# A training-step kernel on one Trainium2 core: the opening reordered, layer-norm statistics six rows ahead instead of eight, and mask products made four wide ones

## The chip, the core and the metric

The kernel runs on one core of one Trainium2 chip. The metric is the device time of one execution in microseconds (us). A measurement has several runs of a kernel, and beside them runs of the kernel before on the same chip. The granted clock is the share of full speed that TensorE was given, as the profile records it; half clock is 0.5. The span in a profile, from the first instruction to the last, is 1 to 3 us shorter than the time of the same run.

## The reference

The kernel computes the output of a two-part layer and the gradients of all its inputs. Only the first part matters here (shortened): layer norm, a two-dimensional FFT, a product with a complex weight, and the inverse FFT.

```python
def _A_ref(x, w_r, w_i):                       # x: 2048 x 448
    X = rfft2(x.astype(float32), axes=(-2, -1))
    X = X * (w_r + 1j * w_i)
    return irfft2(X, s=(S, D), axes=(-2, -1)).astype(bfloat16)

h  = x + _A_ref(_layernorm(x), w_r, w_i)
h2 = h + _B_ref(_layernorm(h), w1, b1, w2, b2) # two matrix products and a gelu
...
_out, _vjp = jax.vjp(_f, A_x, A_w_r, A_w_i, B_w1, B_b1, B_w2, B_b2)
return (_out, *_vjp(grad_out))
```

## The kernel before

FFTs are done as matrix products with tables of sines and cosines. The kernel opens with a *row stage*: a loop over 16 tiles of 128 rows of x. For each tile, VectorE needs the mean and variance of the rows (`ln_stats`), a table scaled by their reciprocal standard deviation (`scale_R`, tile `rX`), and the sums and differences of the row's halves (`fold_prep`, tile `rS`, two rows at a time). With these TensorE does a row product (`row_a`), and four iterations later a second one (`row_b`). Products of grad_out with w2 (`fill`) stand in between, so that TensorE has work while VectorE prepares the next row. They need only loads.

The reciprocal root for rows 6 to 15 is a chain of ten small operations on GpSimd, for two rows at a time:

```python
def newton_gp(v, y, sl):
    ...
    gp_.tensor_scalar(out=v, in0=v, scalar1=LN_EPS, scalar2=None, op0=ALU.add)
    gp_.tensor_scalar(out=yi, in0=v.bitcast(I32), scalar1=-0.5, scalar2=RSQRT_MAGIC, op0=ALU.mult, op1=ALU.add)
    for c0, c1 in RSQRT_STEPS:
        gp_.tensor_tensor(out=a, in0=y, in1=y, op=ALU.mult)
        gp_.tensor_tensor(out=a, in0=a, in1=v, op=ALU.mult)
        gp_.tensor_scalar(out=a, in0=a, scalar1=c0, scalar2=c1, op0=ALU.mult, op1=ALU.add)
        gp_.tensor_tensor(out=y, in0=a, in1=y, op=ALU.mult)
```

Two tables say in which iteration `t` the statistics of a row (`STATS`) and the GpSimd root of a pair (`GROUPS`) are issued. In the kernel before the statistics of row t+8 are issued in iteration t:

```python
GROUPS = {0: (6, 8), 1: (8, 10), 3: (10, 12), 5: (12, 14), 7: (14, 16)}
STATS = {0: (6, 7), 1: (8, 9), **{t: (t + 8,) for t in range(2, 8)}}
...
for t in range(NT):
    ...
    if t + 1 < NT:
        row_a(t + 1, Rs.pop(t + 1))
    fill(FILL_A[t])
    if 1 <= t and t + 3 < NT:
        ...
        Rs[t + 3] = scale_R(t + 3)
    row_b(t - 3)
    ...
    if t % 2 and t < 12:
        fold_prep(xn, t // 2 + 2)
    for i in STATS.get(t, ()):
        ln_stats(xn, i, mvx)
    for _ in range(3 if t > 0 else 0):
        if next(uv, None):                     # a piece of the group tables
            break
    if t in GROUPS:
        a, b = GROUPS[t]
        newton_gp(mvx[:, a:b, 1], rstd_x[:, a:b], slice(a, b))
    ...
    fill(FILL_B[t])
```

The tables for the next stage (`Ut`, `Vt`) are also made during this loop. Each column is multiplied by a mask, in eight narrow products per table, on whichever of VectorE and ScalarE has less work by the kernel's own account:

```python
for j in range(4):
    m = msk[:, j:j + 1]
    dj = d1[:, :, :, j - 1] if j else dst[:, :, 112:128]
    for o, c in ((d0[:, :, :, j], 0), (dj, 1)):
        if load[1] + 0.24 < load[0] + 0.38:
            ve.tensor_scalar(out=o, in0=cv[:, :, :, c], scalar1=m, scalar2=None, op0=ALU.mult)
        else:
            sc.activation(out=o, in_=cv[:, :, :, c], func=ACT.Copy, scale=m)
        yield
```

## Time and profile before

| | before |
|---|---|
| median time | 356.7 us (356.2 to 357.64, 3 runs) |
| span of the profiled run, mean granted clock | 355.7 us, 0.989 |
| row product of row 4 starts | 19.97 us |
| row product of row 14 starts | 40.85 us |
| first product of the stage after (permI with Vt) starts | 50.37 us |

The last rows come from the timeline of TensorE. The busy shares, the windows and the waits of the kernel before stand in the prediction. Columns are start, time, engine, line, operation, output and inputs, and the number of instructions; a bracket gives the idle time just before and what ended it. ScalarE's timeline of before:

```profile
28.26 1.93 ACT L82 ACTIVATE Ut<-rO,cols 128x256 bf16<-128x256 bf16 x3
29.93 0.69 ACT L82 CAST rS<-ps_ff 128x512 bf16<-128x512 f32 x1
```

TensorE's timeline of before, at the same time:

```profile
30.67 0.57 PE L218 MATMUL ps_ff<-csF,rS 112*128 112x226 bf16 x4 [1.62 <-ACT rS L82]
```

Three mask products in a row hold ScalarE for 1.93 us. The copy of a row product out of PSUM, which the program also names `rS`, stands behind them, and TensorE waits 1.62 us for it.

GpSimd's timeline of before, from the last reciprocal root (rows 14 and 15), which begins at 32.97 us:

```profile
33.33 0.29 POOL L1174 TENSOR_SCALAR stats<-mvx 128x16 f32<-128x16 f32 x1
33.68 0.33 POOL L1176 TENSOR_SCALAR stats<-mvx 128x16 f32<-128x16 f32 x1
...
36.30 0.19 POOL L388 TENSOR_TENSOR rstd_x<-nt_f,rstd_x 128x2 f32<-128x2 f32 x1
```

### The profile page before, as it was taken

To read this page: it belongs to the slowest core of one execution; us is meant where nothing else is said; L and a number is where in the kernel's file an instruction comes from. 1 tells how busy PE (TensorE), PEld (TensorE's weight loads), DVE (VectorE), ACT (ScalarE), POOL (GpSimd) and SP (SyncE) were. 2 spreads that over 40 slices of the span, in tenths; PEclk is the share of its full clock that TensorE was granted. 3 is DMA by queue.
4 is the path that set the end of the run, shared out by engine and by line. 5 is a ranking of instruction groups with operands and counts; after the bars stand their busy time and mean duration, and the time that the engine had idled before them with its cause. 6 is when DMAs were issued, how large, how long until landed. Compare 5 with 4: busy or idle time off the path is not lost.

```text
span 355.7 us, 6447 instructions
## 1 busy us (share of the span) xinstructions
PE 341.0 (96%) x2133; PEld 183.8 (52%) x2133; DVE 254.5 (72%) x680; ACT 213.6 (60%) x457; POOL 69.1 (19%) x227
## 2 busy tenths in 40 slices
PE   5888999999999999999999999999999999999995
PEld 2345765555645555555555555544454544565542
DVE  5797638981884888776235888786595965499993
ACT  4549848965986545504222345566387866579872
POOL 8667100000221000001001111110000000067860
PEclk9699999999999999999999999999999999999999
DMA  8999969758999999977777999989966898799995
GB/s 209 272 186 211 235 172 184 161 163 284 280 292 357 299 350 237 251 218 222 183 186 150 190 213 189 216 151 300 292 180 194 231 232 248 228 203 265 245 282 218
DMA packets 147672, 81.62 MB, mean 229 GB/s; under 512 B 95480, under 2 KB 139768, under 8 KB 147384
## 3 DMA queue, kind: packets, MB, share of 16 engines
q1 hardware_dynamic: 147352, 80.83, 91.5%
q10 hardware_dynamic: 288, 0.39, 0.3%
q8 instruction: 16, 0.26, 0.3%
q14 instruction: 16, 0.13, 0.2%
HBM read 27.56 MB, written 23.89 MB: 145 GB/s over the span
## 4 chain that ended last, share of the span: by engine, by line
PE 73%; DVE 8%; ACT 7%; DMA 5%; issue 2%; SPq 2%; POOL 0%; DVEq 0%; ACTq 0%
PE ps_mm L218 61%; PE ps_ff L218 12%; DVE r L82 4%; DMA out_dram<-rG 2%; ACT rO L82 2%; DMA rB<-in_A_w_i_dram 2%; ACT rG L82 2%; DVE stats L82 2%; DMA rA<-in_A_x_dram 2%; SPq L297 1%; ACT Ut L82 1%; DVE rA L82 1%; DVE rS L82 1%; ACT rX L82 1%; ACT Vt L82 1%
## 5 line engine op out<-in xcount | busy, mean ns | idle before, releaser
L218 PEld LDWEIGHTS <-r 128*128 128x128 bf16 (+1 forms) x660 | 61.8, 104 | 49.6 <-issue 2.5
L218 PEld LDWEIGHTS <-rS 128*128 128x128 bf16 (+2 forms) x496 | 40.5, 98 | 38.3 <-issue 5.9
L218 PE MATMUL ps_mm<-rD,r 128*128 128x448 bf16 x224 | 44.5, 352 | 0.0
L82 ACT CAST rO<-ps_mm 128x512 bf16<-128x512 f32 (+1 forms) x66 | 35.2, 579 | 11.3 <-PE ps_mm L218 10.8
L218 PE MATMUL ps_mm<-rC,rE 128*128 128x448 bf16 x144 | 35.9, 370 | 3.6 <-DMA rC<-in_grad_out_dram 3.6
L218 PEld LDWEIGHTS <-rst 128*128 128x128 bf16 (+1 forms) x320 | 23.8, 97 | 29.0 <-issue 13.7
L218 PE MATMUL ps_mm<-r,rst 128*128 128x512 bf16 (+3 forms) x192 | 36.5, 353 | 0.0
L82 ACT CAST r<-ps_ff 128x452 bf16<-128x452 f32 x56 | 31.8, 575 | 7.6 <-PE ps_ff L218 7.4
L218 PE MATMUL ps_mm<-rB,r 128*128 128x448 bf16 x160 | 31.2, 352 | 0.1
L218 PE MATMUL ps_mm<-rG,rst 128*128 128x512 bf16 (+1 forms) x128 | 28.4, 380 | 0.0
L82 ACT ACTIVATE r<-ps_mm,rstd_h 128x448 bf16<-128x448 f32 x16 | 10.1, 633 | 26.8 <-PE ps_mm L218 26.8
L82 ACT ACTIVATE r<-rC 128x448 bf16<-128x448 bf16 x16 | 9.1, 571 | 26.7 <-DMA out_dram<-r 21.6
L82 DVE SCALAR_TENSOR_TENSOR r<-ps_mm,b2col,r 128x448 bf16<-128x448 f32 x16 | 10.9, 683 | 19.9 <-PE ps_mm L218 18.4
L82 ACT ACTIVATE rG<-rG 128x896 bf16<-128x896 bf16 x14 | 13.3, 950 | 14.9 <-DVE rG L82 14.7
L218 PEld LDWEIGHTS <-rO 128*128 128x128 bf16 (+1 forms) x165 | 15.6, 98 | 11.5 <-DMA rO<-in_B_w_dram 1.1
L218 PE MATMUL ps_mm<-rE,rS 128*128 128x448 bf16 x112 | 21.5, 352 | 0.0
L1182 POOL TENSOR_SCALAR lcol<-lcol 128x1 f32<-128x1 f32 x16 | 8.5, 530 | 64.7 <-ACT r L82 64.7
L218 PEld LDWEIGHTS <-rE 128*128 128x128 bf16 x148 | 14.4, 101 | 12.3 <-issue 5.6
L218 PE MATMUL ps_mm<-rC,rO 128*128 128x448 bf16 x80 | 19.1, 352 | 0.8 <-DMA rO<-in_B_w_dram 0.8
L1373 POOL TENSOR_SCALAR lcol<-lcol 128x1 f32<-128x1 f32 x16 | 4.7, 296 | 77.0 <-ACT r L82 76.9
L218 PE MATMUL ps_ff<-csI,rAT 113*128 113x224 bf16 (+1 forms) x108 | 19.0, 298 | 0.6 <-ACT rAT L82 0.4
L82 ACT CAST rG<-ps_mm 128x512 bf16<-128x512 f32 (+1 forms) x28 | 14.4, 550 | 8.1 <-PE ps_mm L218 8.0
(197 smaller groups left out, 661.0 us busy)
## 6 DMA issues: line engine op xcount, KB each, us to landing
out_dram<-rO SPq DMA_DIRECT2D x34, 256.0 KB
r<-in_B_w_dram SPq DMA_DIRECT2D x5, 1024.0 KB
r<-r SPq DMA_DIRECT2D x16, 226.0 KB
r<-r SPq DMA_DIRECT2D x32, 113.0 KB
rS<-in_B_w_dram SPq DMA_DIRECT2D x4, 896.0 KB
out_dram<-rG SPq DMA_DIRECT2D x10, 256.0 KB
rO<-in_B_w_dram SPq DMA_DIRECT2D x2, 1024.0 KB
w_d<-rG SPq DMA_DIRECT2D x1, 1808.0 KB
```

The costliest lines, as they stand in the source:

```text
L82: fn(**kw)
L218: nc.tensor.matmul(out, lhsT=lhsT, rhs=rhs, start=start, stop=stop)
L297: nc.sync.dma_start_transpose(out=wT, in_=B_w2[j * P:(j + 1) * P, :].rearrange("f (t c) -> f t c", c=P))
L1182: gp_.tensor_scalar(out=m1, in0=ms, scalar1=-1.0 / D, scalar2=None, op0=ALU.mult)
L1373: gp_.tensor_scalar(out=m1, in0=ms, scalar1=-2.0 / D, scalar2=None, op0=ALU.mult)
```

## The change

Its intent: have the sine tables and the first statistics done sooner, keep TensorE's clock up with more idle matmuls, issue the statistics later so that VectorE, which is full from 20 to 31 us, gets to the tables and folds of the next rows first, and take the mask products off ScalarE.

```diff
-    for _ in range(12):
+    for _ in range(26):
         nc.tensor.matmul(idle[:, 0:D], lhsT=rAT[:, 0:P], rhs=rAT[:, 0:D], start=True, stop=True)
 ...
-            for j in range(4):
-                m = msk[:, j:j + 1]
-                ...
+            for out, c, j in ((d0, 0, 0), (d1, 1, 1)):
+                n = 4 - j
+                load[1] += 0.06 + 256.0 * n / 960.0
+                nc.vector.tensor_tensor(out=out, in0=cv[:, :, :, c:c + 1].broadcast_to([P, 16, 16, n]),
+                                        in1=mskb[:, 0:1, 0:1, j:4].broadcast_to([P, 16, 16, n]), op=ALU.mult)
+                yield True
+            evac_mask(dst[:, :, 112:128], cv[:, :, :, 1], msk[:, 0:1])
+            yield
 ...
-    for fn in fwd_ops[:4]:
+    for fn in fwd_ops:                 # both sine tables before the first statistics
         fn()
 ...
-    GROUPS = {0: (6, 8), 1: (8, 10), 3: (10, 12), 5: (12, 14), 7: (14, 16)}
-    STATS = {0: (6, 7), 1: (8, 9), **{t: (t + 8,) for t in range(2, 8)}}
+    GROUPS = {0: (6, 8), 3: (8, 10), 5: (10, 12), 7: (12, 14), 9: (14, 16)}
+    STATS = {0: (6, 7), **{t: (t + 6,) for t in range(2, 10)}}
 ...
-    FILL_A = (3, 3, 3, 3, 3, 3, 3, 3, 3, 3, 3, 3, 3, 3, 3, 3)
-    FILL_B = (3, 3, 3, 3, 3, 3, 3, 3, 3, 3, 3, 3, 3, 3, 3, 3)
+    FILL_A = (4, 4, 4, 3, 3, 4, 4, 4, 4, 4, 4, 3, 3, 3, 3, 3)
+    FILL_B = (0, 0, 0, 3, 3, 3, 3, 3, 3, 3, 3, 3, 3, 3, 3, 3)
```

Cut from this: the load of x rows 2 and 3 goes ahead of the first part of grad_out, `fold_prep` of rows 2 and 3 and the identity go ahead of row 0, and four fills stand before row 0 in place of six after it.

More of the change, by code (lines that the diff above doesn't have):

```diff
@@ L310 @@
     load_w2T()
+    nc.sync.dma_start(out=xn[:, 2:4, :], in_=x_pt[:, 2:4, :])
     load_go(0)
-    nc.sync.dma_start(out=xn[:, 2:4, :], in_=x_pt[:, 2:4, :])
     load_go(1)
@@ L463, with evac_mask @@
     comp_ring = ring(rO, 0, 2, 512)
+    mskb = mem.tile([P, 1, 1, 4], BF16, name="mskb")
+    def evac_mask(out, in_, m):
+        if load[1] + 0.43 < load[0] + 0.7:
+            ve.tensor_scalar(out=out, in0=in_, scalar1=m, scalar2=None, op0=ALU.mult)
+        else:
+            load[0] += 0.3
+            sc.activation(out=out, in_=in_, func=ACT.Copy, scale=m)
     def gen_UV():
@@ L469, in gen_UV @@
         msk, mk, k0, k1 = masks(gp_, c_, f_)
+        gp_.tensor_copy(out=mskb[:, 0, 0, :], in_=msk)
         slf = col()
@@ L502, in gen_UV @@
             d1 = dst[:, :, 64:112].rearrange("p g (l f) -> p g l f", f=3)
-            for j in range(4):
-                m = msk[:, j:j + 1]
-                dj = d1[:, :, :, j - 1] if j else dst[:, :, 112:128]
-                for o, c in ((d0[:, :, :, j], 0), (dj, 1)):
-                    if load[1] + 0.24 < load[0] + 0.38:
-                        ve.tensor_scalar(out=o, in0=cv[:, :, :, c], scalar1=m, scalar2=None, op0=ALU.mult)
-                    else:
-                        sc.activation(out=o, in_=cv[:, :, :, c], func=ACT.Copy, scale=m)
-                    yield
+            for out, c, j in ((d0, 0, 0), (d1, 1, 1)):
[6 more added lines that the diff above has]
+            yield
     Rp = rO[:, 1536:1536 + P]
@@ L852 @@
         fn()
-    for fn in fwd_ops[:4]:
+    for fn in fwd_ops:
         fn()
+    nc.vector.memset(csF[:, 0, :, 0:1], 0.0)
     sc.activation(out=warm, in_=eps_x, func=ACT.Sqrt)
@@ L869 @@
     fold_prep(xn, 0)
+    ve.tensor_scalar(out=ident[:], in0=krow[:, 0:P], scalar1=pcol, scalar2=None, op0=ALU.is_equal)
     ve.reciprocal(out=rstd_x[:, 0:2], in_=rstd_x[:, 0:2])
@@ L874 @@
     sc.activation(out=rstd_x[:, 2:4], in_=mvx[:, 2:4, 1], func=ACT.Sqrt, bias=eps_x, scale=1.0)
-    for fn in fwd_ops[4:6]:
-        fn()
+    fold_prep(xn, 1)
     ve.reciprocal(out=rstd_x[:, 2:4], in_=rstd_x[:, 2:4])
-    for fn in fwd_ops[6:]:
-        fn()
-    nc.vector.memset(csF[:, 0, :, 0:1], 0.0)
     Rs.update({t: scale_R(t) for t in range(2, 4)})
-    ve.tensor_scalar(out=ident[:], in0=krow[:, 0:P], scalar1=pcol, scalar2=None, op0=ALU.is_equal)
     gp_.memset(W_view_F[:, :, :, DF:KW], 0.0)
@@ L887 @@
     gen_inv_cols(1)
+    fill(4)
     row_a(0, Rs.pop(0))
-    fold_prep(xn, 1)
     for t in (4, 5):
@@ L893 @@
         fn()
-    fill(6)
+    fill(0)
     turn_biases = load_biases()
     Meter.side, Meter.every, Meter.count = [], 1, 0
-    GROUPS = {0: (6, 8), 1: (8, 10), 3: (10, 12), 5: (12, 14), 7: (14, 16)}
-    STATS = {0: (6, 7), 1: (8, 9), **{t: (t + 8,) for t in range(2, 8)}}
+    GROUPS = {0: (6, 8), 3: (8, 10), 5: (10, 12), 7: (12, 14), 9: (14, 16)}
+    STATS = {0: (6, 7), **{t: (t + 6,) for t in range(2, 10)}}
     INV_S = {11: 0, 12: 1, 13: 2, 14: 3}
```

## The prediction

> **What bounds the kernel now.** I read the page first (busy shares, then the slices), then the table of windows over the opening, then the waits of TensorE, then the timeline of the row stage (the loop over 16 row tiles, up to about 47 us).
>
> ```profile
> PE 341.0 (96%) x2133; PEld 183.8 (52%) x2133; DVE 254.5 (72%) x680; ACT 213.6 (60%) x457; POOL 69.1 (19%) x227
> PEclk9699999999999999999999999999999999999999
> ```
>
> TensorE is busy for 96% of the span; outside the opening nearly nothing is left to win. PEclk shows one dip, in the second slice. So I cut the opening into windows.
>
> ```profile
> 0.00:10.00 10.00, 6.03 (x20) 2.56 (x21) 5.26 (x28) 3.67 (x6) 8.04 (x46) 1.00 0.85 219
> 10.00:20.00 10.00, 7.81 (x35) 3.32 (x33) 8.68 (x35) 6.02 (x14) 5.51 (x22) 0.66 1.22 252
> 20.00:31.00 11.00, 8.77 (x67) 5.45 (x68) 10.96 (x40) 7.79 (x16) 8.33 (x33) 1.00 1.02 181
> 31.00:46.00 15.00, 14.95 (x128) 10.36 (x126) 9.31 (x27) 12.39 (x25) 4.28 (x19) 1.00 1.00 220
> ```
>
> After the stretch and its length, the columns are busy time of PE, weight loads, VectorE, ScalarE, GpSimd, then clock, DMA share, GB/s. From 20 to 31 us VectorE is full (10.96 of 11) and PE is not; from 31 us PE is full. From 10 to 20 us PE has a clock of 0.66 and the DMA share is over 1. The opening is thus bound by loads, then by VectorE, then by PE.
>
> ```profile
> PE ps_mm L218 <- DMA rC<-in_grad_out_dram: 3.6, 3, 2.5
> PE ps_ff L218 <- DVE rS L82: 1.8, 2, 1.1
> PE ps_ff L218 <- ACT rS L82: 1.6, 1, 1.6
> PE ps_ff L218 <- DVE rX L82: 0.8, 2, 0.5
> ```
>
> These waits (total, times, longest) are what the change aims at: grad_out not yet landed, folds (rS) and scaled tables (rX) late on VectorE, and one ScalarE stall at 29 to 30.7 us behind three mask products of 0.65 us each.
>
> The landings recorded in the trace set a floor: x rows 0-1 at 3.7, first w2 block 6.05, grad_out quarters 9.18, 10.92, 13.27, 14.48, x rows 2-3 at 9.75, rows 4-7 at 12.09, second w2 block 16.80, rows 8-11 at 18.52, third block 21.37, rows 12-15 at 22.95, fourth block 26.99 us. None of these transfers waits for compute.
>
> **What the Trainium skill says.**
> - "TensorE: Matmul & The Clock Gate", Part 1: the clock is gated to half by default and judged over free-running windows of 3413 ns. The trace agrees: full clock from 6.64, half for 6.83 us from 10.06, full from 16.88; the idle matmuls start every 374 ns, which is 448 columns at 1.2 GHz.
> - "ScalarE: Activation LUTs", What ACT_TABLE_LOAD costs: about 1283 ns per load. The loads here take 1.28 us.
> - "VectorE: DVE Perf Modes", Mode 2x_1P: two bf16 results per cycle need step 1. The new product repeats each element of cv with step 0, so I take one per cycle at 0.96 GHz, an estimate from this page: 1024 elements 1.07 us, 768 elements 0.80 us, plus 0.06. No instruction in the trace has this form.
> - "GPSIMD Engine Reference", 1. Specifications: the SBUF interfaces are shared with VectorE and contended when VectorE reads two SBUF inputs or uses both ports. The trace agrees:
>
> ```profile
> 26.38 0.68 DVE L82 TENSOR_TENSOR rS<-rA 128x448 bf16<-128x448 bf16 x2
> ...
> 26.17 0.24 POOL L383 TENSOR_SCALAR rstd_x<-mvx 128x2 int32<-128x2 int32 x1
> 26.50 0.61 POOL L385 TENSOR_TENSOR nt_f<-rstd_x 128x2 f32<-128x2 f32 x1
> 27.19 0.20 POOL L386 TENSOR_TENSOR nt_f<-nt_f,mvx 128x2 f32<-128x2 f32 x1
> ```
>
> A GpSimd step that takes 0.19 us alone takes 0.61 when it begins under a fold and ends with it.
>
> **The change, part by part.**
>
> *Idle matmuls, 12 to 26.* They start at 1.21; cold until a window closes (6.6 at the same phase) is 14 at 374 ns, the other 12 at 189 ns: done at about 8.9. PE now first waits for the first grad_out quarter, which the swap with x rows 2-3 puts at about 9.75, so the idle matmuls delay nothing. The clock should stay full from about 6.6. Before, half speed at 10 to 16.9 us stretched work that waited for loads anyway: little gain.
>
> *Tables first.* Two scalar and two tensor operations of 452 floats (0.65 + 1.1 us) go before the first statistics, and the memset of csF waits for the second sine; the first statistics start at about 6.0 instead of 3.7. Scaled tables 2 and 3 come at about 11.4 instead of 14.2 us. Then rows 4-5 wait only for their landing at 12.09: statistics 1.4, the nine-step rsqrt on VectorE 1.7, statistics of rows 6-7 1.4, scaled table 0.15, fold 0.6: row 4 ready at 17.3 us, against 19.97 when its product ran before. PE reaches it early (16 fills and 4 rows are done at 15.4). So here it leads by 2.6 us. A sine table load (1.28 us) moves from 11.5 to about 19 us on ScalarE; four PSUM buffers should absorb it.
>
> *Masks.* Sixteen mask products (11 on ScalarE at 0.54, 5 on VectorE at 0.34) become four wide products (1.13, 0.86, twice) on VectorE and two on ScalarE: ScalarE minus 4.8 us, VectorE plus 2.3. The 1.6 us ScalarE stall goes.
>
> *Statistics six rows ahead.* Statistics and GpSimd rsqrt of a pair now end two iterations before the scaled table needs them, not four. In VectorE order this is a loop: scaled table 0.15, fold 0.60, statistics of the odd row of the next pair 0.54, aggregation 0.25, GpSimd rsqrt, scaled table. The rsqrt is 10 steps 0.275 apart, 2.75 us. Period without interference: 1.54 + 0.1 + 2.75 + 0.1 = 4.5 us per two rows. PE needs per row 7 fills x 0.189 + 0.22 + 0.39 = 1.93, so 3.9 per two rows: the loop is slower than PE. And the wide masks fall inside those rsqrts: each holds a GpSimd step for about its length less 0.28, so 0.85 and 0.6 us.
>
> From row 4 on: rsqrt of rows 6-7 runs 16.7 to 20.2 (fold and table operations hold it 0.7), row 6 ready 21.0; rows 8-9: 21.9 to 25.5 with a mask, row 8 ready 26.4 (PE is there at 24.7); rows 10-11: 27.2 to 30.5, row 10 ready 31.4; rows 12-13: 32.2 to 35.2, row 12 ready 36.1; rows 14-15, with two further operations and two masks: 36.9 to 41.7, row 14 ready 42.6. Before, the product of row 14 ran at 40.85 with two fills more done (0.38), so equal progress is 40.47. Loss 2.1 us. Without the masks' holds row 14 is ready at 39.5: gain 1.0 us. From row 14 on, and after the row stage, the order on PE is the same and PE-bound, so this difference goes through to the end. Removed work alone is worth at most 1.9 us: the 49th fill cannot start before the fourth w2 block (26.99), and 13.1 us of work stand before it (48 fills, 9 first and 5 second row products), so at least 13.9 us are lost there, against 15.8 us lost by 45.6 us now (29.8 us of work at full clock).
>
> **Rivals.**
> 1. *The GpSimd loop takes the place of the removed waits* (worked out above): +1 to +2 us. For it: the loop in the instruction order, and 0.61 against 0.19 us above. Against it: the holds depend on where each mask falls.
> 2. *The waits simply go:* the start leads by 2.6 us and masks no longer stall PE; then the w2 landings are the bound: -1 to -1.9 us, 355 us. For it: the fill counts (16 before row 4) fit the landings closely, as if tuned. Against it: the loop of 4.5 us.
> 3. *All is hidden behind loads:* DMA shares over 1 to 20 us, nothing changed in their order but one swap; +-0.4 us. Against it: PE idles for VectorE and ScalarE too, 4.2 us in the waits above.
>
> **Range and chances.** I give rival 1 somewhat more weight than rival 2: 0.55 x (+1.8) + 0.45 x (-1.0) = +0.5, rounded up for the late table load: 356.7 + 0.6 = 357.3 us. Range 355.2 (rival 2 in part, plus the spread of 1.4 us seen before) to 359.5 (full holds and some). Two per cent is 7.1 us, beyond the floor by far: faster 0.01, same 0.97, slower 0.02.
>
> **What would show it.** Right: VectorE waits for GpSimd rstd_x at rows 8, 10, 12, 14, PE for VectorE rS at row products 8, 10, 14, rsqrts of 3.3 us or more under the masks; clock full from about 7 us; the ScalarE stall gone; four mask products of about 1.1 and 0.86 us. Wrong: PE waiting in the row stage only for w2 landings; masks at half those times; GpSimd steps of 0.19 us under a mask; or a shift of the whole PE order after 50 us, which I hold to be untouched.

## The result and the profile after

| | before | after |
|---|---|---|
| median time | 356.81 us (356.2 to 357.64, 4 runs) | 362.88 us (361.09 to 362.91, 4 runs) |
| span of the profiled run | 355.7 us | 361.0 us |
| row 4 starts | 19.97 us | 16.75 us |
| row 14 starts | 40.85 us | 43.50 us |
| first product with Vt starts | 50.37 us | 54.74 us |

The ratio is 1.0156, with a 95% interval of 1.0119 to 1.0193. The change makes the kernel slower by some 6 us. That is still within 2%, but above the predicted range (355.2 to 359.5 us).

The four runs of after had spans of 361.0, 361.1, 361.1 and 359.3 us. The last was the only one with a mean granted clock of 1.0 (the others had 0.995, 0.986 and 0.995). Only the profiled run, one of those with 0.995, shows where the clock fell.

First the page of after, busy shares and the clock of the 40 slices:

```profile
PE 344.3 (95%) x2147; PEld 185.0 (51%) x2147; DVE 255.6 (71%) x676; ACT 211.5 (59%) x451; POOL 73.1 (20%) x228
PEclk9999989999999999999999999999999999999999
```

The dip of the clock in the second slice is gone. A new one stands in the sixth slice, from 45 to 54 us. Now the windows (stretch and its length, busy time of PE, weight loads, VectorE, ScalarE, GpSimd, then clock, DMA share, GB/s):

```profile
0.00:10.00 10.00, 8.79 (x38) 4.15 (x39) 8.36 (x38) 4.93 (x9) 6.19 (x36) 1.00 0.85 215
10.00:20.00 10.00, 6.53 (x49) 3.89 (x47) 8.16 (x33) 5.63 (x14) 8.10 (x39) 1.00 1.09 271
20.00:31.00 11.00, 9.04 (x65) 5.24 (x62) 7.59 (x22) 7.41 (x15) 5.88 (x23) 1.00 1.01 211
31.00:46.00 15.00, 11.24 (x81) 6.78 (x81) 8.65 (x26) 7.31 (x15) 6.86 (x25) 0.94 0.89 188
```

The stretch from 20 to 31 us shows what the change aimed at: VectorE falls from 10.96 to 7.59 us. The loss is in the next one. From 31 to 46 us TensorE is at work for 11.24 us instead of 14.95, and its clock falls to 0.94, while no other engine is full. Some chain of waits sets the pace there.

The waits of TensorE in after (total, times, longest):

```profile
PE ps_ff L218 <- DVE rS L82: 7.2, 7, 2.0
PE ps_mm L218 <- DMA rC<-in_grad_out_dram: 1.8, 2, 1.3
```

The waits for grad_out have halved and the ScalarE stall is gone. In their place TensorE waits 7.2 us for folds, against 1.8 before; 5.0 us of it falls between 20 and 48 us, where before has none (its wait of 1.08 us ends at 19.97). What a fold waits for is in VectorE's timeline of after:

```profile
23.48 1.24 DVE L516 TENSOR_TENSOR Ut<-rO,mskb 128x1024 bf16<-128x1024 bf16 x1
26.20 0.26 DVE L82 TENSOR_SCALAR rX<-Rm,rstd_x 128x128 bf16<-128x128 bf16 x1 [1.48 <-POOL rstd_x L388]
...
37.92 1.22 DVE L516 TENSOR_TENSOR Vt<-rO,mskb 128x1024 bf16<-128x1024 bf16 x1
39.06 0.28 DVE L82 TENSOR_SCALAR rX<-Rm,rstd_x 128x128 bf16<-128x128 bf16 x1
39.23 0.95 DVE L516 TENSOR_TENSOR Vt<-rO,mskb 128x768 bf16<-128x768 bf16 x1
42.84 0.32 DVE L82 TENSOR_SCALAR rX<-Rm,rstd_x 128x128 bf16<-128x128 bf16 x1 [2.67 <-POOL rstd_x L388]
43.07 0.68 DVE L82 TENSOR_TENSOR rS<-rA 128x448 bf16<-128x448 bf16 x2
```

VectorE stands idle for the GpSimd root in each pair of rows: 1.48 us before row 8's table, 2.67 us before row 14's, and the fold comes after the table. GpSimd, in turn, in after:

```profile
37.71 0.24 POOL L382 TENSOR_SCALAR mvx<-mvx 128x2 f32<-128x2 f32 x1 [1.73 <-DVE mvx L82]
38.03 1.25 POOL L1180 TENSOR_SCALAR stats<-mvx 128x16 f32<-128x16 f32 x1
39.35 0.96 POOL L1182 TENSOR_SCALAR stats<-mvx 128x16 f32<-128x16 f32 x1
40.39 0.19 POOL L383 TENSOR_SCALAR rstd_x<-mvx 128x2 int32<-128x2 int32 x1
```

GpSimd was itself idle for 1.73 us, waiting for VectorE's statistics. So each engine waits for the other in turn. And two operations that took 0.29 and 0.33 us before now take 1.25 and 0.96 us: each begins under a wide mask product (37.92 to 39.14, 39.23 to 40.18) and ends about 0.1 us after it. The last root runs from 37.71 to 42.81, 5.1 us against 3.52 before.

The first root is late for another reason. GpSimd, in after, much earlier:

```profile
6.03 0.41 POOL L339 IOTA r<- 128x256 f32 x1 [2.52 <-DVE r L871]
```

Its index arithmetic for the mask tables waits here for a small VectorE operation that now stands behind both sine tables; in before it starts at 3.61 us. It is done at 17.78 us, 15.83 before, and the first root starts only then, at 17.86, though VectorE had the statistics ready at 16.26.

TensorE's timeline of after, at that place:

```profile
43.50 0.64 PE L218 MATMUL ps_ff<-rX,rS 128*128 128x128 bf16 x4 [1.96 <-DVE rS L82]
43.98 1.24 PE L218 MATMUL ps_mm<-rC,rE 128*128 128x448 bf16 x3
...
47.32 0.47 PE L218 MATMUL ps_ff<-rX,rS 128*128 128x128 bf16 x4
47.62 0.73 PE L218 MATMUL ps_mm<-rC,rE 128*128 128x448 bf16 x3
```

After the wait of 1.96 us three fills take 1.24 us instead of 0.73. The trace records half clock from 44.07 to 47.48 us. From row 14 to row 15 it is 3.82 us here and 2.18 us before (40.85 to 43.03).

To see where the 5.3 us of span came from, I counted matmuls from the end of both traces and compared when the same one starts. After is ahead by 1.9 us where before is at 31 us. It is behind by 0.7 us at 40. At the row-14 product it is behind by 3.0 us (2.65 us later, and two fills of 0.19 us fewer done), at 49 us by 4.7, from 85 us to the end by 5.3. So the sum is about 3.0 for the row stage, 1.6 for the half clock (3.82 less 2.18) and a rest of some 0.7, of which 0.6 comes between 49 and 85 us.

### The profile page after: what moved, and what is told of

It is laid out like the page before. It is cut to its first block, busy times and chain, and to the rows that moved or that the text cites. A ratio compares the mean times of both kernels' runs of the same rounds, so it can differ in the third digit from the quotient of the medians.

```text
span 361.0 us, 6469 instructions
## 1 busy us (share of the span) xinstructions
PE 344.3 (95%) x2147; PEld 185.0 (51%) x2147; DVE 255.6 (71%) x676; ACT 211.5 (59%) x451; POOL 73.1 (20%) x228
## 4 chain that ended last, share of the span: by engine, by line
PE 77%; POOL 7%; DVE 5%; ACT 5%; issue 3%; DMA 2%; SPq 1%; DVEq 0%; ACTq 0%; POOLq 0%
PE ps_mm L218 65%; PE ps_ff L218 12%; ACT rO L82 2%; DMA rB<-in_A_w_i_dram 2%; ACT rG L82 2%; DVE r L82 1%; DVE rS L82 1%; POOL nt_f L387 1%; DVE rA L82 1%; ACT rX L82 1%; POOL nt_f L386 1%; POOL cols L406 1%; DVE stats L82 1%; POOL rstd_x L388 1%; POOL nt_f L385 1%
## 5 line engine op out<-in xcount | busy, mean ns | idle before, releaser
L218 PE MATMUL ps_mm<-rC,rE 128*128 128x448 bf16 x144 | 34.5, 361 | 1.9 <-DMA rC<-in_grad_out_dram 1.8
L82 ACT CAST rS<-ps_ff 128x512 bf16<-128x512 f32 x31 | 18.0, 581 | 9.6 <-PE ps_ff L218 9.4
```

The costliest lines, as they stand in the source:

```text
L82: fn(**kw)
L218: nc.tensor.matmul(out, lhsT=lhsT, rhs=rhs, start=start, stop=stop)
```

## The experiments

My theory was a loop: table, fold, statistics, GpSimd root, next table. With statistics only six rows ahead, each root begins when the previous pair's fold and the statistics behind it are done, and the wide masks lengthen the roots. The rivals were the new opening order (sine tables before statistics, another order of loads) and the wide masks as plain work on VectorE. The experiments undo one part of after or do one part in before. The first four share 7 runs of before with a median of 357.46 us.

### e1: after, with statistics eight rows ahead

```diff
-    GROUPS = {0: (6, 8), 3: (8, 10), 5: (10, 12), 7: (12, 14), 9: (14, 16)}
-    STATS = {0: (6, 7), **{t: (t + 6,) for t in range(2, 10)}}
+    GROUPS = {0: (6, 8), 1: (8, 10), 3: (10, 12), 5: (12, 14), 7: (14, 16)}
+    STATS = {0: (6, 7), 1: (8, 9), **{t: (t + 8,) for t in range(2, 8)}}
```

> The changed kernel with only the statistics and GpSimd rsqrt put back to eight rows ahead. Loop theory (statistics six rows ahead make the chain statistics, GpSimd rsqrt, scaled table, fold, statistics set the pace of the row stage): TensorE no longer waits about 2 us for the fold before row 14, the clock stays full, and the time falls to 355.5 to 357.5 us. Rival (the wide masks and VectorE's load themselves cost the time): it stays at 360 us or more.

Measured: 355.92 us (355.75 to 356.19), ratio to before 0.9965 [0.9934, 0.9996]. Row 14 starts at 38.41 us, the first product with Vt at 47.94. These two lines of the schedule turn a loss of 6 us into a gain of about 1 us. The new opening and the wide masks are both still in, so neither can be the loss by itself.

### e2: before, with statistics six rows ahead

```diff
-    GROUPS = {0: (6, 8), 1: (8, 10), 3: (10, 12), 5: (12, 14), 7: (14, 16)}
-    STATS = {0: (6, 7), 1: (8, 9), **{t: (t + 8,) for t in range(2, 8)}}
+    GROUPS = {0: (6, 8), 3: (8, 10), 5: (10, 12), 7: (12, 14), 9: (14, 16)}
+    STATS = {0: (6, 7), **{t: (t + 6,) for t in range(2, 10)}}
```

> The kernel before with only the statistics and GpSimd rsqrt put to six rows ahead. Loop theory: row 14's product slips from 40.9 to about 43 to 44 us, the time becomes 359 to 361 us although no mask changed. Rival (masks are the cause): within 1 us of the kernel before.

Measured: 359.16 us (358.96 to 359.25), ratio 1.0054 [1.0028, 1.008]. The time is as expected; row 14 was expected at 43 to 44 us and starts at 41.86, only 1.0 later than in before. The roots now begin 4.5 to 5.1 us apart (18.40, 23.48, 27.94, 32.84, 37.64), and GpSimd waits 1.73 us for VectorE before each of the last four. GpSimd's timeline of e2, the start of the second:

```profile
23.48 0.23 POOL L382 TENSOR_SCALAR mvx<-mvx 128x2 f32<-128x2 f32 x1 [1.73 <-DVE mvx L82]
```

In before they begin 3.0 to 3.6 us apart (19.56, 22.58, 25.88, 29.50, 32.97), with no such wait after the first. So the loop exists without any wide mask, and costs 1.9 us (0.0054 x 357) there.

### e3: after, with the sixteen narrow masks

```diff
-            for out, c, j in ((d0, 0, 0), (d1, 1, 1)):
-                ... nc.vector.tensor_tensor(...)       # wide product
-            evac_mask(dst[:, :, 112:128], cv[:, :, :, 1], msk[:, 0:1])
+            for j in range(4):
+                ...                                    # the narrow products of before
```

> The changed kernel with the sixteen narrow masks back. Loop theory with holds: the two wide masks no longer hold GpSimd operations for about 1 us each, row 14 about 2 us earlier than in the changed kernel, 358 to 359.5 us. Rival (masks alone are the cause): 356 us or less. Rival (holds do not matter): as the changed kernel, 361 to 363 us.

Measured: 358.61 us (358.41 to 358.85), ratio 1.004 [1.0013, 1.0066]. Row 14 starts at 41.10 us, 2.4 earlier than in after. The last root takes 3.47 us (36.88 to 40.35) instead of 5.1. The wide masks cost about 4 us in after (362.88 less 358.61), though they make less work in all. But the loss isn't all theirs: 1.4 us against before (0.004 x 357) is left. At row 14 e3 is behind by 0.6 us (41.10 less 40.47, which is 40.85 less two fills); the rest comes after the row stage.

### e4: before, with the four wide masks

```diff
-            for j in range(4):
-                ...                                    # the narrow products
+            for out, c, j in ((d0, 0, 0), (d1, 1, 1)):
+                ... nc.vector.tensor_tensor(...)       # wide product
+            evac_mask(dst[:, :, 112:128], cv[:, :, :, 1], msk[:, 0:1])
```

> The kernel before with only the four wide mask products. Loop theory: GpSimd runs two pairs ahead here, so its holds are hidden, and ScalarE's stall of 1.6 us goes: 355 to 357 us. Rival (masks are the cause): 359 us or more.

Measured: 357.56 us (355.48 to 358.31), ratio 1.0001 [0.9958, 1.0044]. No gain can be seen, and the time lies above the expected 355 to 357 us. The last root takes 5.12 us (33.75 to 38.87), as long as in after, yet row 14 starts at 39.56 us, 1.3 sooner than in before. The same root of 5.1 us costs TensorE a wait of only 0.54 us where it starts 4 us earlier. With e1, that rules out the wide masks as plain work. How much of the 1.3 us lasts to the end is not settled: the four runs took 355.48, 356.83, 358.3 and 358.31 us.

### e5: after, with idle matmuls in the wait before row 14

For this and the next three, 7 runs of before gave a median of 357.23 us.

```diff
     for t in range(NT):
+        if t == 13:
+            again = ps_ff()
+            for _ in range(10):
+                nc.tensor.matmul(again[:, 0:D], lhsT=rAT[:, 0:P], rhs=rAT[:, 0:D], start=True, stop=True)
```

> The changed kernel with ten idle matmuls (1.9 us at full clock) put on TensorE where it waits 2 us for the fold of rows 14 and 15. Clock theory: the wait itself stays (row 14 still near 43.5 us), but the half clock of 3.41 us after it goes, so all runs fall to the level of the one run at full clock: 361.0 to 361.5 us. Rival (the half clock is not due to this wait, or costs nothing): 362.5 to 363 us, or more by the idle work.

Measured: 361.27 us (360.91 to 362.31), ratio 1.0117 [1.0095, 1.0138]. TensorE's timeline of e5:

```profile
41.20 2.06 PE L918 MATMUL ps_ff<-rAT 128*128 128x448 bf16 x10
43.32 0.64 PE L218 MATMUL ps_ff<-rX,rS 128*128 128x128 bf16 x4
43.80 0.73 PE L218 MATMUL ps_mm<-rC,rE 128*128 128x448 bf16 x3
...
45.55 0.39 PE L218 MATMUL ps_ff<-rX,rS 128*128 128x128 bf16 x4
```

Row 14 starts about when it did, as it must: its fold is no earlier. But the three fills behind it take 0.73 us again, and row 15 follows after 2.23 us instead of 3.82. The clock was full from 21.44 us to the end. So the half clock after the wait is a cost of its own, 1.6 us here. The time points the same way: the ratio falls from 1.0156 to 1.0117, which is 1.4 us, but the intervals overlap, and one of e5's two runs with a mean clock of 1.0 took 362.31 us.

A mean clock below 1.0 alone doesn't tell of this cost. The profiled run of e5 has a half clock too, from 18.03 to 21.44 us, and that of e1 from 17.36 to 20.78, and e1 is faster than before all the same. A likely reason, not tested, is that TensorE still has other waits to come there, and few from row 14 on.

### e6: after, with the two 128x16 operations on VectorE

```diff
-    gp_.tensor_scalar(out=xcol[:, 0, :], in0=mvx[:, :, 0], scalar1=-1.0, scalar2=None, op0=ALU.mult)
+    ve.tensor_scalar(out=xcol[:, 0, :], in0=mvx[:, :, 0], scalar1=-1.0, scalar2=None, op0=ALU.mult)
...
-    gp_.tensor_scalar(out=xcol[:, 2, :], in0=mvx[:, :, 0], scalar1=-2.0 / D, scalar2=None, op0=ALU.mult)
+    ve.tensor_scalar(out=xcol[:, 2, :], in0=mvx[:, :, 0], scalar1=-2.0 / D, scalar2=None, op0=ALU.mult)
```

These are the two that took 1.25 and 0.96 us in the last root.

> The changed kernel with the two 128x16 operations that GpSimd ran between the steps of the last rsqrt (1.25 and 0.96 us) moved to VectorE, at their late place in the program. Theory of holds (whatever GpSimd runs under a wide mask waits for its end): rsqrt steps take their place under the masks, and only about 0.6 us of row 14's delay goes, more only if the half clock goes with it: 360.5 to 362.5 us. Rival (these two operations are 2.2 us of their own work): 2.2 us or more earlier, 358 to 360.5 us.

Measured: 360.61 us (360.28 to 361.41), ratio 1.0097 [1.0077, 1.0117]. The last root takes 4.46 us (37.73 to 42.19), and row 14 starts at 42.88 us, only 0.6 earlier. Taking the two away does not take the holds away, because the next steps of the root come under the masks instead. The profiled run had no half clock after row 14. Of the 2.3 us gained on after (362.88 less 360.61) the wait is 0.6, and the clock the likely rest; this run doesn't separate them.

### e7: after, with statistics seven rows ahead

```diff
-    GROUPS = {0: (6, 8), 3: (8, 10), 5: (10, 12), 7: (12, 14), 9: (14, 16)}
-    STATS = {0: (6, 7), **{t: (t + 6,) for t in range(2, 10)}}
+    GROUPS = {0: (6, 8), 2: (8, 10), 4: (10, 12), 6: (12, 14), 8: (14, 16)}
+    STATS = {0: (6, 7), 2: (8, 9), **{t: (t + 7,) for t in range(3, 9)}}
```

> The changed kernel with statistics seven rows ahead (rows 8 and 9 together at t=2), rsqrt three iterations ahead of its use instead of two. Loop theory: with a third iteration the rsqrt of a pair no longer follows in VectorE order the scaled table of the pair before, so the loop is open, and row 5 is not behind the statistics of rows 8 and 9 as with eight rows ahead: 354.5 to 356 us. Rival (each row of distance costs alike): half way, 358 to 360 us.

Measured: 355.05 us (354.85 to 356.28), ratio 0.9945 [0.9923, 0.9967]. This is the fastest version, ahead of both kernels. Row 14 starts at 37.30 us, and the clock is full in every run. GpSimd's timeline of e7, the last root:

```profile
31.51 0.25 POOL L382 TENSOR_SCALAR mvx<-mvx 128x2 f32<-128x2 f32 x1
32.86 1.04 POOL L385 TENSOR_TENSOR nt_f<-rstd_x 128x2 f32<-128x2 f32 x1
33.98 0.95 POOL L386 TENSOR_TENSOR nt_f<-nt_f,mvx 128x2 f32<-128x2 f32 x1
36.40 0.20 POOL L388 TENSOR_TENSOR rstd_x<-nt_f,rstd_x 128x2 f32<-128x2 f32 x1
```

The root is held by the masks as before, 5.1 us from 31.51 to 36.60. But it begins 6.2 us sooner, without a wait for VectorE: no bracket stands on the first line, where after has 1.73 us. The waits of TensorE in e7:

```profile
PE ps_ff L218 <- DVE rS L82: 2.6, 3, 1.6
```

The folds cost 2.6 us in place of 7.2, and between 20 and 48 us only 0.4 in place of 5.0. One row of lead opens the loop.

### e8: before, with the new opening order alone

```diff
+    nc.sync.dma_start(out=xn[:, 2:4, :], in_=x_pt[:, 2:4, :])
     load_go(0)
-    nc.sync.dma_start(out=xn[:, 2:4, :], in_=x_pt[:, 2:4, :])
...
-    for fn in fwd_ops[:4]:
+    for fn in fwd_ops:
         fn()
+    nc.vector.memset(csF[:, 0, :, 0:1], 0.0)
...
-    for fn in fwd_ops[4:6]:
-        fn()
+    fold_prep(xn, 1)
...
-    for fn in fwd_ops[6:]:
-        fn()
-    nc.vector.memset(csF[:, 0, :, 0:1], 0.0)
...
     row_a(0, Rs.pop(0))
-    fold_prep(xn, 1)
```

The identity also moves up, as in the change. Idle matmuls, masks, statistics and fills are those of before.

> The kernel before with only the order of the opening changed: tables first, rows 2 and 3 of x before the first quarter of grad_out, fold of rows 2 and 3 early. Landings theory: row 4 about 2.5 us earlier, but VectorE, the ScalarE stall and the w2 landings bound what follows: 0 to 1.9 us gained against the kernel before. Rival (tables first is what costs): 358 us or more with the kernel before at 357.

Measured: 355.67 us (355.54 to 357.48), ratio 0.9972 [0.9941, 1.0003]. Row 4 starts at 18.60 us, 1.4 earlier than in before and not the expected 2.5 (TensorE waits 1.88 us for w2 ahead of it), row 14 at 38.66. The opening order is no loss. It looks like a gain of 1 us, though the interval just reaches no difference.

### e9: e7, with weight copies starting one step later

A remainder of some 0.7 us arises after the half clock. In after TensorE waits 0.9 us there for copies that ScalarE makes of its results, and in ScalarE's timeline these stand behind weight copies that wait for a load. The next four runs had 11 runs of before beside them, median 357.38 us.

```diff
-                if make_inv and c2 >= 3:
+                if make_inv and c2 >= 4:
```

> Seven rows ahead, and the copies of the loaded filter weights begin one step later (at c2=4). The traces show ScalarE waiting for the weights' landing inside such a copy while two evacuations for TensorE stand behind it (0.9 us of waits in the changed kernel and with seven rows, 0.2 in the kernel before). If that is where about 0.8 us of the lead after the row stage goes: 354.0 to 354.8 us against 355.0 with seven rows alone. If it isn't: 355 us or more.

Measured: 356.18 us (355.7 to 357.09), ratio 0.9965 [0.9944, 0.9987]. The expected gain didn't come. The waits of TensorE in e9 from 40 to 100 us:

```profile
PE ps_ff L218 <- DVE r L82: 0.6, 1, 0.6
PE ps_ff L218 <- ACT rX L82: 0.5, 2, 0.4
```

The wait for ScalarE halved (it is 1.0 us in e7), and a new one for VectorE took its place. This is a miss, and the cause of the 0.7 us stays open.

### e10: e7, with the narrow masks

```diff
-            for out, c, j in ((d0, 0, 0), (d1, 1, 1)):
-                ... nc.vector.tensor_tensor(...)       # wide product
+            for j in range(4):
+                ...                                    # the narrow products of before
```

> Seven rows ahead, with the sixteen narrow masks. Loop theory: with the loop open the holds of the wide masks are hidden, so the wide masks are worth ScalarE's stall of 1 to 1.6 us or nothing: 355 to 356.5 us. Rival (holds of the wide masks still cost): under 354.8 us.

Measured: 356.48 us (356.37 to 356.79), ratio 0.9974 [0.9953, 0.9996]. The waits of TensorE in e10:

```profile
PE ps_ff L218 <- ACT rS L82: 1.5, 1, 1.5
```

The stall on ScalarE is back. Seven rows ahead the wide masks are worth about 1 us (0.9974 less 0.9945, times 357; the intervals overlap); six rows ahead they cost 4 (after against e3). And e3 and e10, both with narrow masks, differ only in one row of lead: it is worth 2.4 us (1.004 less 0.9974, times 357). That is what the loop costs with no wide mask in it.

### e11: e7, with 12 idle matmuls

```diff
-    for _ in range(26):
+    for _ in range(12):
```

> Seven rows ahead, with 12 idle matmuls as before. If the idle matmuls are worth little, as predicted, since the slow stretch waits for loads anyway: 355 to 355.6 us. If they are worth half of the half-clock stretch (6.83 us in the kernel before): 356.5 to 358 us.

Measured: 355.55 us (354.96 to 357.43), ratio 0.9956 [0.9931, 0.9982]. The half clock is back from 8.71 to 12.13 us, and the time is the same as e7's within the intervals.

### e12: before, with six rows ahead and the wide masks

```diff
-    GROUPS, STATS = ...                                # eight rows ahead
+    GROUPS, STATS = ...                                # six rows ahead, as in e2
...
-            for j in range(4):
-                ...                                    # the narrow products
+            for out, c, j in ((d0, 0, 0), (d1, 1, 1)):
+                ... nc.vector.tensor_tensor(...)       # wide product, as in e4
```

> The kernel before with both suspects together, statistics six rows ahead and the wide masks, and nothing else of the change. Loop theory with holds: alone they cost 1.7 and 0.1 us, together more than their sum, since the masks hold the rsqrt only where it sets the pace: row 14 near 44.5 us, 360.5 to 363.5 us. Rival (costs add): 358.5 to 359.5 us.

Measured: 363.86 us (362.93 to 365.13), ratio 1.0182 [1.0151, 1.0212]. Alone they cost 1.9 and 0.0 us; together 6.5 us (0.0182 x 357). The time lies just above the expected range, and whether it is 2% slower than before is unclear. Row 14 starts at 44.72 us, and half clock follows from 44.85 to 48.26. Before needs nothing but these two parts to become as slow as after, or slower. Some of it is not the loop: TensorE also waits 2.3 us for w2 loads in e12, against 0.8 in before and none in after. What delays them there I did not pursue.

## Why the prediction was right or wrong

The loop of rival 1 was right, and it is what happened. What failed is the step that carries its wait through to the end at full clock, and with it the time: of the 5.3 us of span, 2.1 were in the sum for rival 1, and row 14 added 0.9, the half clock 1.6 and a rest without a known cause 0.7. By the prediction's steps:

- *Row 4's lead.* Predicted at 17.3 us, it started at 16.75. The lead was real, and after was still 1.9 us ahead at 31 us.
- *Idle matmuls.* "Little gain" was right (e11, seven rows ahead). The first part of grad_out landed at 8.58 us and not at 9.75, so the idle matmuls held the first fill for 0.16 us.
- *Masks.* The two forms take 1.24 and 0.95 us, predicted 1.13 and 0.86: the fixed part is about 0.16 us rather than 0.06. The ScalarE stall went, as said.
- *The loop.* The prediction put its period without interference at 4.5 us. In e3, without wide masks, roots begin 4.5 to 4.9 us apart. The holds are as described and a little longer: the two operations under the masks take 0.96 and 0.63 us more than before, predicted 0.85 and 0.6. VectorE waits for the root at rows 6, 8, 10, 12 and 14, and TensorE for the folds. Row 14 was predicted ready at 42.6 us and began at 43.50. Of these 0.9 us most was there from the start: the first root began at 17.86 instead of 16.7 us, because GpSimd was busy with its index arithmetic until 17.78, against 15.83 in before. The prediction overlooked that "tables first" holds this work up (by 2.4 us at its start, shown with the result). The last root took 5.1 us instead of 4.8. A late first root stays late in a loop, as each root waits for the one before.
- *"Without the masks' holds row 14 is ready at 39.5: gain 1.0 us."* Wrong: e3 has row 14 at 41.10 us, a loss of 0.6. The loop costs time even with no wide mask in it (e3 against e10), and the late first root (18.01 us instead of 16.7) is 1.3 of the 1.6 us missed.
- *"From row 14 on ... this difference goes through to the end."* This step failed. It took TensorE's clock to be full from about 7 us on, and so carried the wait on without loss. The wait before row 14 let the clock fall to half for 3.41 us, and this cost 1.6 us more. e5 shows it: with the same wait and no half clock behind it, row 15 follows 1.6 us sooner. A further 0.7 us is not explained: e9, built on one reading of it, gained nothing, and the version with narrow masks (e3) loses some 0.7 us after the row stage too.
- *Range and chances.* The working gave +2.1 us for rival 1; the prediction then put 1.8 for it, weighed it against rival 2 (-1.0 us) and came to +0.6. But the two were not equally founded. The loop had been read off the instruction order and timed step by step; rival 2 was only the hope that nothing takes the removed waits' place. The sum for rival 1 should have stood, with a wider upper end, though it alone (358.8 us) would still have been 4 us short. Measured, its term was mis-sized too: 3.0 us at row 14 in place of 2.1, then 1.6 and 0.7 us that were not in the sum.

The floor set by w2 landings played no part: after reached no fill that had to wait for them.

The gain that the change aimed at exists. e7 has every part of it but the six rows, and is 2 us faster than before. The statistics' short lead lost it, and the wide masks inside the roots made the loss larger.

## What to carry to other kernels

When a producer is moved later to free an engine, follow the whole cycle that it belongs to, through every engine back to itself, and compare its period with the consumer's. Here one row of lead decided between 2 us won and 6 us lost, and two edits that cost 2 and 0 us alone cost 6.5 together. If the cycle is slower than the consumer, count what follows the consumer's waits as well: a wait of 2 us took another 1.6 us through the clock.

## What the Trainium skill lacked or had wrong

- "TensorE: Matmul & The Clock Gate", Part 1, has the clock go back to half after at least one idle window of about 3.4 us. Here a wait of 1.96 us was enough in the profiled run of after, and again in e12. In the 3.41 us ahead of the half clock (40.66 to 44.07, taking the window to end where the record begins) TensorE was at work from 40.66 to 41.55 and from 43.50 on, some 1.5 us. So, if the window lies there, it need not be idle throughout. The length of the wait alone doesn't decide: half clock followed waits of 1.60 us (e1), 1.64 (e3) and 1.73 (e5) before row 4, but not one of 1.58 there in e7 or one of 1.88 in e8.
